# Causal mask by identity matmul, constant rows filled by DMA, V loads from GpSimd, and one-batch FFN groups in a fused attention and FFN kernel

## The chip, the cores and the metric

The kernel runs on 1 core of a Trainium2 chip. The metric is device time in microseconds (us). The profile records one execution. A run is called slow when it lies more than 1.5% above the fastest run of the same kernel; comparisons use fast runs, and differences in us are between means of fast runs. Ratios are the mean time of one kernel's fast runs over the mean of the other's fast runs in the same rounds, so they are not quite the ratio of the times quoted beside them. The kernel before itself took 329.7 to 331.4 us in the several rounds, so a difference between kernels of different rounds is uncertain by some 2 us.

Engine names in profile lines: PE is TensorE, PEld its weight loads, DVE VectorE, ACT ScalarE, POOL GpSimd, SP SyncE. A name with a q (SPq, ACTq) is that engine's sequencer, which here issues transfers.

## The reference

Eight batches of eight heads, 576 positions, head width 64. Attention with a decay from cumulated log f and a causal mask is followed by an FFN with a three-tap convolution and a gate. Abridged:

```python
scores = scale * np.matmul(q, k.transpose(0, 1, 3, 2))
cum = np.cumsum(np.log(np.clip(f, 0.0001, 1.0)), axis=-1)
decay = cum[:, :, :, None] - cum[:, :, None, :]
scores = np.where(causal, -1e9, scores + decay)       # causal: strictly above the diagonal
attn = softmax(scores)
x = np.matmul(attn, v)        # heads put side by side: (8, 576, 512)
h = np.maximum(x @ w_in, 0.0)                         # 512 -> 1024
conv_out = sum(conv_w[k] * shifted(h, k) for k in range(3))
out = (h * sigmoid(conv_out)) @ w_out                 # 1024 -> 512
```

## The kernel before

Work goes by groups of four heads (`hb`, 16 of them) and head pairs (`i`, 32). The q and k of a group are transposed on their way in by a DMA that lays each value into an odd row of a 128-row bf16 tile; the even rows hold what the DMA finds beside it and must become constants. A clamp (a multiply and an add on the 16-bit pattern) does this. Two of the even rows then get the high and low part of cumulated log f, so that one matmul gives score and decay. A ring of four tiles holds the groups.

```python
    def clamp(hb, p, side, eng):
        t = (stq_t, stk_t)[side][hb % RING].bitcast(U16)[:, 2 * p * S:2 * (p + 1) * S]
        eng.tensor_scalar(t, t, lim[:, 2 * side:2 * side + 1], lim[:, 2 * side + 1:2 * side + 2],
                          op0=ALU.mult, op1=ALU.add)

    def rows_of(hb):                       # the rows of cumulated log f, from DRAM
        nc.gpsimd.dma_start(tq[0:1, 0:HS], kd[0:1, c, :].rearrange("j h s -> j (h s)"))
        nc.gpsimd.dma_start(bass.AP(tensor=tk.tensor, ...), kd[:, c, :]...)

    def load_v(b, eng, h0=0, h1=H):        # five DMAs; eng is ScalarE for batch 0, SyncE later
        ...
    # [cut] a mask is a select on GpSimd after the exponential
    def diag_exp(i):
        p_of[i, 3] = pd_pool.tile([128, 1024], FP32, name="p32")
        nc.scalar.activation(p_of[i, 3], sc_of.pop((i, 2)), AF.Exp, scale=SCALE)

    def diag_mask(i):
        p_of[i, 2] = pm_pool.tile([128, 1024], FP16, name="pm")
        nc.gpsimd.affine_select(p_of[i, 2]..., p_of.pop((i, 3))..., pattern=[[0, 8], [1, 128]], base=0,
                                channel_multiplier=-1, compare_op=ALU.is_ge, fill=0.0)
    # [cut] the FFN takes batches in groups (first batch, number)
    GROUPS = [(0, 1), (1, 2), (3, 2), (5, 2), (7, 1)]
```

The order on each engine is fixed when the program is built: each piece of work is a `task` with an estimated cost, the tasks it follows and a key, and a small list scheduler plays them through once.

The softmax here doesn't subtract the row's maximum and nothing guards it: scores larger than these inputs give would overflow.

## Time and profile before

| | before |
|---|---|
| median of 3 runs | 331.68 us (329.85 to 332.91) |
| span of the profiled run | 329.2 us |
| busy PE / DVE / ACT / POOL | 231.0 / 238.5 / 202.3 / 163.4 us |
| first exponential of attention | 23.7 us |

Two parts of the page come back throughout. The first line gives busy time, share of the span and instruction count of each engine. The others give, for each DMA queue, its packets, its megabytes and the time that its packets took as a share of 16 engines' span. Queue q1 carries what SyncE issues, q10 what ScalarE issues, q0 what GpSimd issues.

```profile
PE 231.0 (70%) x2296; PEld 147.6 (45%) x2296; DVE 238.5 (72%) x260; ACT 202.3 (61%) x300; POOL 163.4 (50%) x179
...
q1 hardware_dynamic: 127526, 40.28, 60.9%
q0 software_dynamic: 2528, 2.31, 4.1%
q10 hardware_dynamic: 4872, 1.34, 2.0%
```

Packets in flight together count each in full, so in a short stretch the share can exceed 1.

### The profile page before, as it was taken

Reading aid. Unit: us, or ns where it says so; the run is one execution under the profiler, and the core shown is the slowest. Engines: PE = TensorE matmul, PEld = TensorE weight load, DVE = VectorE, ACT = ScalarE, POOL = GpSimd, SP = SyncE. Lnnn points to the kernel's source line nnn. Section 1 sums busy time; section 2 is a strip of 40 time slices with the busy share of each in tenths; the row PEclk is TensorE's granted clock in tenths of the full one; section 3 lists DMA queues with packets and bytes.
Section 4 is the critical chain, followed back from the end, with each engine's and each line's share of the span. In section 5 each row is a group of like instructions: output and inputs, shape, how many; then the busy total and the mean of one; then the engine's idle time right before and its main releaser. Section 6 shows DMA issues by size and latency. Waiting matters only on the chain. (4 is left out here: it accounts for less than half of the span.)

```text
span 329.2 us, 5881 instructions
## 1 busy us (share of the span) xinstructions
PE 231.0 (70%) x2296; PEld 147.6 (45%) x2296; DVE 238.5 (72%) x260; ACT 202.3 (61%) x300; POOL 163.4 (50%) x179
## 2 busy tenths in 40 slices
PE   0018267567588995196285995699889988889994
PEld 0016155445365663163143663365557554445441
DVE  1606147879897379999999889199956997986720
ACT  2106066569676893275477687098887976565632
POOL 0847262859666749379299989962242100000000
PEclk9999689899879999589699899599999999999998
DMA  9999999779279699669935899411050110121323
GB/s 160 272 190 219 215 216 194 129 118 176 50 119 218 120 205 269 109 105 248 209 60 100 165 215 194 81 65 66 20 149 3 66 64 0 66 96 65 129 112 128
DMA packets 134954, 44.31 MB, mean 135 GB/s; under 512 B 128545, under 2 KB 129709, under 8 KB 134926
## 3 DMA queue, kind: packets, MB, share of 16 engines
q1 hardware_dynamic: 127526, 40.28, 60.9%
q0 software_dynamic: 2528, 2.31, 4.1%
q10 hardware_dynamic: 4872, 1.34, 2.0%
q8 instruction: 18, 0.29, 0.4%
q14 instruction: 10, 0.08, 0.1%
HBM read 14.00 MB, written 9.58 MB: 72 GB/s over the span
## 5 line engine op out<-in xcount | busy, mean ns | idle before, releaser
L368 PE MATMUL mm<-xt,w_in_f 128*128 128x384 f16 (+1 forms) x416 | 77.0, 320 | 8.7 <-ACT ht L381 3.1
L420 PE MATMUL mm<-w_out_f,hg 128*128 128x512 f16 (+1 forms) x296 | 71.7, 391 | 3.3 <-ACT ht L389 2.1
L260 ACT ACTIVATE po<-sc 128x1024 f16<-128x1024 f32 x64 | 64.1, 1028 | 10.5 <-PE sc L254 10.2
L278 POOL TENSOR_SCALAR_AFFINE_SELECT pm<-p 128x1024 f16<-128x1024 f32 x32 | 40.8, 1275 | 46.5 <-ACT p L274 46.5
L398 DVE SCALAR_TENSOR_TENSOR u<-ht,cwt 128x1152 f32<-128x1152 f16 (+1 forms) x40 | 53.8, 1345 | 10.3 <-ACT ht L385 5.2
L411 DVE SCALAR_TENSOR_TENSOR hg<-hg,ht 128x1152 f16<-128x1152 f16 (+1 forms) x40 | 55.3, 1386 | 5.5 <-ACT hg L405 5.4
L405 ACT ACTIVATE hg<-u,cwt 128x1152 f16<-128x1152 f32 (+1 forms) x40 | 42.3, 1062 | 27.6 <-DVE u L400 27.6
L368 PEld LDWEIGHTS <-w_in_f 128*128 128x128 f16 x416 | 39.7, 99 | 33.2 <-issue 14.0
L299 PE MATMUL O<-va,pm 128*128 128x65 f16 x256 | 32.9, 201 | 30.3 <-DVE xn L312 15.7
L400 DVE SCALAR_TENSOR_TENSOR u<-ht,cwt,u 128x1152 f32<-128x1152 f16 (+1 forms) x40 | 51.4, 1284 | 0.8
L254 PE MATMUL sc<-stq,stk 128*128 128x448 bf16 (+3 forms) x256 | 41.3, 292 | 14.1 <-ACT po L260 7.6
L100 POOL TENSOR_SCALAR stk<-stk,lim 128x1152 uint16<-128x1152 uint16 x21 | 43.1, 2052 | 8.8 <-DMA stk<-in_k_dram 8.7
L420 PEld LDWEIGHTS <-hg 128*128 128x128 f16 (+1 forms) x296 | 29.0, 100 | 35.0 <-issue 7.2
L429 ACT ACTIVATE ob<-mm 128x512 f32<-128x512 f32 (+1 forms) x34 | 20.2, 595 | 34.7 <-PE mm L420 27.8
L299 PE MATMUL O<-va,po 128*128 128x65 f16 x640 | 39.2, 200 | 0.0
L299 PEld LDWEIGHTS <-po 128*128 128x128 f16 x640 | 33.2, 102 | 10.5 <-issue 9.0
L299 PEld LDWEIGHTS <-pm 128*128 128x128 f16 x256 | 25.1, 103 | 27.8 <-POOL pm L278 19.6
L274 ACT ACTIVATE p<-sc 128x1024 f32<-128x1024 f32 x32 | 33.0, 1032 | 3.7 <-PE sc L269 3.0
L310 DVE RECIPROCAL rc<-O 128x10 f32<-128x10 f32 x32 | 6.8, 213 | 37.6 <-PE O L299 37.6
L254 PEld LDWEIGHTS <-stk 128*128 128x128 bf16 x256 | 20.4, 104 | 26.8 <-issue 18.2
L100 POOL TENSOR_SCALAR stq<-stq,lim 128x1152 uint16<-128x1152 uint16 x17 | 27.5, 1618 | 0.1
L312 DVE TENSOR_TENSOR xn<-O,rc 128x640 f16<-128x640 f32 x32 | 26.4, 825 | 1.1
(71 smaller groups left out, 248.6 us busy)
## 6 DMA issues: line engine op xcount, KB each, us to landing
out_dram<-ob SPq DMA_DIRECT2D x16, 512.0 KB, 2.8
vf<-in_v_dram SPq DMA_DIRECT2D x28, 256.0 KB, 5.1
vf<-in_v_dram ACTq DMA_DIRECT2D x8, 128.0 KB, 4.8
w_in_f<-in_moe_w_in_dram POOLq DMA_DIRECT2D x1, 1024.0 KB, 9.6
w_out_f<-in_moe_w_out_dram POOLq DMA_DIRECT2D x1, 1024.0 KB, 11.1
vf<-in_v_dram SPq DMA_DIRECT2D x7, 128.0 KB, 5.2
out_dram<-ob SPq DMA_DIRECT2D x3, 256.0 KB, 3.0
xt<-xn SPq DMA_TRANSPOSE x30, 2.6
```

What stands on the lines that cost most here:

```text
L100: eng.tensor_scalar(t, t, lim[:, 2 * side:2 * side + 1], lim[:, 2 * side + 1:2 * side + 2], op0=ALU.mult, op1=ALU.add)
L254: nc.tensor.matmul(sc[:, OFF[m]:OFF[m] + w], tk[:, h * S + 128 * m:h * S + 128 * (m + 1)], tq[:, h * S + 128 * (m + 1):(h + 1) * S], start ...
L260: nc.scalar.activation(p_of[i, s][:, 0:1024], sc_of.pop((i, s)), AF.Exp, scale=SCALE)
L274: nc.scalar.activation(p_of[i, 3], sc_of.pop((i, 2)), AF.Exp, scale=SCALE)
L278: nc.gpsimd.affine_select(p_of[i, 2].rearrange("p (m j) -> p m j", j=128), p_of.pop((i, 3)).rearrange("p (m j) -> p m j", j=128), pattern= ...
L299: nc.tensor.matmul(O[:, s, 65 * Q:65 * (Q + 1)], w, va[:, h, m, :], start=(m == 0), stop=(m == Q))
L368: nc.tensor.matmul(ps[:, 0:w], w_in_f16[:, cc, 128 * ff:128 * (ff + 1)], xt[:, cc, w * t:w * (t + 1)], start=(cc == 0), stop=(cc == NCC - 1))
L398: nc.vector.scalar_tensor_tensor(u, hl, cwt[:, ff, 0:1], hc, op0=ALU.mult, op1=ALU.add)
L400: nc.vector.scalar_tensor_tensor(u, hr, cwt[:, ff, 1:2], u, op0=ALU.mult, op1=ALU.add)
L405: nc.scalar.activation(hgt[g, ff].rearrange("p (a s) -> p a s", s=S), u_of.pop((g, ff)), AF.Tanh, scale=cwt[:, ff, 2:3])
L411: nc.vector.scalar_tensor_tensor(hv, hv, 1.0, hc, op0=ALU.add, op1=ALU.mult)
L420: nc.tensor.matmul(ps[0:n, :], hgt[g, ff][:, 128 * c:128 * c + n], w_out_f16[:, ff, :], start=(ff == 0), stop=(ff == NFF - 1))
```

## The change

The intent is to free GpSimd, and DVE, whose steps are stretched beside it (the prediction shows this). The mask moves to PE: an identity matmul writes a matrix of 0 and -1e6 into PSUM, and the scores accumulate on it. From the fifth group on, the even rows are no longer clamped but overwritten by a DMA from a constant tile (a fill). V loads are issued from GpSimd. FFN groups are mostly of one batch. The start is rearranged.

```diff
-    GROUPS = [(0, 1), (1, 2), (3, 2), (5, 2), (7, 1)]
+    GROUPS = [(0, 1), (1, 1), (2, 1), (3, 1), (4, 2), (6, 1), (7, 1)]
+    def fill(hb, side):
+        t, src = ((stq_t, zq_src), (stk_t, zk_src))[side]
+        t = t[hb % RING]
+        row = t.shape[-1]
+        nc.sync.dma_start(bass.AP(tensor=t.tensor, offset=int(t.offset), ap=[[2 * row, 64], [1, HS]]), src)
-    nc.scalar.dma_start(fsb, f.rearrange("b h s -> (b h) s"))
+    nc.sync.dma_start(fsb, f.rearrange("b h s -> (b h) s"))
     load_qk(0, 0, 2)
     load_qk(0, 2, 2)
-    load_v(0, nc.scalar, 0, HH)
+    load_v(0, nc.gpsimd, 0, HH)
 ... [cut: constants; clamps of the first group on DVE, each pair followed by its row copies]
-    load_v(0, nc.scalar, HH, H)
-    load_qk(1, 0, 4)
+    load_v(0, nc.gpsimd, HH, H)
+    load_qk(1, 0, 4)
 ... [cut: diagonal scores; the tail likewise]
+            nc.tensor.matmul(sc[:, 512 * s:512 * (s + 1)], identb, trib, start=True, stop=False, ...)
             for m in range(4):
                 nc.tensor.matmul(sc[:, 512 * s + 128 * m:512 * s + 128 * (m + 1)],
-                                 tk[:, o:o + 128], tq[:, o:o + 128], start=True, stop=True)
+                                 tk[:, o:o + 128], tq[:, o:o + 128], start=False, stop=m == 3, ...)
-    def diag_mask(i):
-        nc.gpsimd.affine_select(...)
+    def fill_sources():
+        nc.gpsimd.memset(zq_src, 0.0)
+        nc.gpsimd.memset(zk_src, 0.0)
+        nc.gpsimd.memset(zq_src[0:3, :], 1.0)
+        nc.gpsimd.memset(zk_src[0:1, :], -1.0)
+    CLAMPS = 4
+            if hb >= CLAMPS:
+                even.append(task({"SP": 0.6}, [t_fsrc, x], ..., lambda hb=hb, s=s: fill(hb, s), ...))
+            elif hb:
+                even.extend(task({"DVE": 0.55}, [x], ..., lambda ...: clamp(hb, p, s, nc.vector)) for p in range(2))
-                          key + 0.2, lambda b=b: load_v(b, nc.sync), lag=2.0, dma=5.0)
+                                     key + 1.2, lambda b=b: load_v(b, nc.gpsimd), lag=2.0, dma=5.5, behind=last)
```

More of the change, by code (lines that the diff above doesn't have):

```diff
@@ L61 @@
     ident16 = cpool.tile([128, 128], FP16)
+    identb = cpool.tile([128, 128], BF16)
+    trib = cpool.tile([128, 512], BF16)
+    trit = cpool.tile([128, HH * SL], BF16)
+    zq_src = cpool.tile([64, HS], BF16)
+    zk_src = cpool.tile([64, HS], BF16)
     w_in_f16 = cpool.tile([128, NCC, D_FF], FP16)
@@ L101, in clamp, with rows_qk @@
                           op0=ALU.mult, op1=ALU.add)
-    def rows_qk(hb, eng):
+    def rows_qk(hb, eng, h0, nh):
         tq, tk = stq_t[hb % RING], stk_t[hb % RING]
-        c = slice(hb * HH, (hb + 1) * HH)
-        eng.dma_start(tq[0:1, 0:HS], khi_sb[c, :])
-        eng.dma_start(tk[2:3, 0:HS], khi_sb[c, :])
-        eng.dma_start(tk[4:5, 0:HS], klo_sb[c, :])
+        r, c = slice(hb * HH + h0, hb * HH + h0 + nh), slice(h0 * S, (h0 + nh) * S)
+        eng.dma_start(tq[0:1, c], khi_sb[r, :])
+        eng.dma_start(tk[2:3, c], khi_sb[r, :])
+        eng.dma_start(tk[4:5, c], klo_sb[r, :])
+    def fill(hb, side):
[3 more added lines that the diff above has]
+        nc.sync.dma_start(bass.AP(tensor=t.tensor, offset=int(t.offset), ap=[[2 * row, 64], [1, HS]]), src)
     def rows_of(hb):
@@ L136, in cast_v @@
             eng.tensor_scalar(va[:, 2:4, 0:4, 0:64], vf[:, 2:4, 0:4, :], 1.0, 0.0, op0=ALU.mult, op1=ALU.add)
-    nc.scalar.dma_start(fsb, f.rearrange("b h s -> (b h) s"))
+    nc.sync.dma_start(fsb, f.rearrange("b h s -> (b h) s"))
     load_qk(0, 0, 2)
     load_qk(0, 2, 2)
-    load_v(0, nc.scalar, 0, HH)
     nc.gpsimd.iota(lii[:, 0:1], pattern=[[0, 1]], base=0, channel_multiplier=1)
+    load_v(0, nc.gpsimd, 0, HH)
+    nc.gpsimd.memset(trib, -1.0e6)
+    nc.gpsimd.affine_select(trib.rearrange("p (m j) -> p m j", j=128), trib.rearrange("p (m j) -> p m j", j=128),
+                            pattern=[[0, 4], [-1, 128]], base=-1, channel_multiplier=1,
+                            compare_op=ALU.is_ge, fill=0.0)
+    make_identity(nc, ident)
+    nc.gpsimd.tensor_copy(identb, ident)
     nc.vector.memset(one1, 1.0)
@@ L157 @@
     nc.scalar.preload_act_table(AF.Exp)
-    load_v(0, nc.scalar, HH, H)
-    load_qk(1, 0, 4)
     nc.vector.tensor_tensor_scan(cum, one1.broadcast_to((BH, S)), fsb, 0.0, op0=ALU.mult, op1=ALU.add)
-    for t in range(RING):
-        nc.gpsimd.memset(stk_t[t][:, HS:HS + 64], 0.0)
-    clamp(0, 0, 1, nc.gpsimd)
-    clamp(0, 1, 1, nc.gpsimd)
     nc.vector.tensor_scalar(khi_sb, cum, float(-1.0 / SCALE), None, op0=ALU.mult)
@@ L167 @@
                                    op0=ALU.mult, op1=ALU.subtract)
-    clamp(0, 0, 0, nc.vector)
-    clamp(0, 1, 0, nc.vector)
-    rows_qk(0, nc.scalar)
+    for p in range(2):
+        for s in range(2):
+            clamp(0, p, s, nc.vector)
+        rows_qk(0, nc.scalar, 2 * p, 2)
+    for t in range(RING):
+        nc.vector.memset(stk_t[t][:, HS:HS + 64], 0.0)
+    for t in range(2):
+        nc.vector.memset(p4_t[t][:, HH * SL:], 0.0)
+    for t in range(4):
+        nc.vector.memset(po_t[t][:, 1024:], 0.0)
+    load_v(0, nc.gpsimd, HH, H)
+    load_qk(1, 0, 4)
     nc.sync.dma_start(kd[0], khi_sb)
@@ L173 @@
     nc.sync.dma_start(cwrow, moe_conv_w)
-    for t in range(2):
-        nc.gpsimd.memset(p4_t[t][:, HH * SL:], 0.0)
-    for t in range(4):
-        nc.gpsimd.memset(po_t[t][:, 1024:], 0.0)
+    trv = trit.rearrange("p (h j) -> p h j", j=SL)
+    nc.gpsimd.tensor_copy(trv, trib[:, 0:SL].unsqueeze(1).broadcast_to((128, HH, SL)))
     for t in range(3):
@@ L184 @@
         nc.gpsimd.memset(ht_t[t][:, :, HT_W - 1:HT_W], 0.0)
-    make_identity(nc, ident)
     nc.gpsimd.tensor_copy(ident16, ident)
@@ L191 @@
     mm_pool = ctx.enter_context(tc.tile_pool(name="mmp", bufs=2, space=bass.MemoryType.PSUM))
-    pd_pool = ctx.enter_context(tc.tile_pool(name="pdp", bufs=2))
     pm_pool = ctx.enter_context(tc.tile_pool(name="pmp", bufs=2))
@@ L229, in tail_scores @@
         sc = sc_of["t", hb] = sc_pool.tile([128, 1024], FP32, name="sc")
+        nc.tensor.matmul(sc[:, 0:HH * SL], identb, trit, start=True, stop=False, skip_group_check=True)
         for h in range(HH):
@@ L232, in tail_scores @@
             nc.tensor.matmul(sc[:, SL * h:SL * (h + 1)], tk[:, o:o + 128], tq[:, o:o + SL],
-                             start=True, stop=True)
+                             start=False, stop=h == HH - 1, skip_group_check=True)
     def tail_exp(hb):
-        pt = p_of["t", hb] = pd_pool.tile([128, HH * SL], FP32, name="p32t")
-        nc.scalar.activation(pt, sc_of.pop(("t", hb))[:, 0:HH * SL], AF.Exp, scale=SCALE)
-    def tail_mask(hb):
-        nc.gpsimd.affine_select(p4_t[hb % 2][:, 0:HH * SL].rearrange("p (h j) -> p h j", j=SL),
-                                p_of.pop(("t", hb)).rearrange("p (h j) -> p h j", j=SL),
-                                pattern=[[0, HH], [1, SL]], base=0,
-                                channel_multiplier=-1, compare_op=ALU.is_ge, fill=0.0)
+        nc.scalar.activation(p4_t[hb % 2][:, 0:HH * SL], sc_of.pop(("t", hb))[:, 0:HH * SL], AF.Exp, scale=SCALE)
     OFF = {0: 0, 3: 448, 1: 512, 2: 832}
@@ L266, in diag_scores @@
             tq, tk = stq_t[hb % RING], stk_t[hb % RING]
+            nc.tensor.matmul(sc[:, 512 * s:512 * (s + 1)], identb, trib, start=True, stop=False,
+                             skip_group_check=True)
             for m in range(4):
@@ L269, in diag_scores @@
                 nc.tensor.matmul(sc[:, 512 * s + 128 * m:512 * s + 128 * (m + 1)],
-                                 tk[:, o:o + 128], tq[:, o:o + 128], start=True, stop=True)
+                                 tk[:, o:o + 128], tq[:, o:o + 128], start=False, stop=m == 3,
+                                 skip_group_check=True)
     def diag_exp(i):
-        p_of[i, 3] = pd_pool.tile([128, 1024], FP32, name="p32")
-        nc.scalar.activation(p_of[i, 3], sc_of.pop((i, 2)), AF.Exp, scale=SCALE)
-    def diag_mask(i):
         p_of[i, 2] = pm_pool.tile([128, 1024], FP16, name="pm")
-        nc.gpsimd.affine_select(p_of[i, 2].rearrange("p (m j) -> p m j", j=128),
-                                p_of.pop((i, 3)).rearrange("p (m j) -> p m j", j=128),
-                                pattern=[[0, 8], [1, 128]], base=0,
-                                channel_multiplier=-1, compare_op=ALU.is_ge, fill=0.0)
+        nc.scalar.activation(p_of[i, 2], sc_of.pop((i, 2)), AF.Exp, scale=SCALE)
     def pv(i, s):
@@ L461, in task @@
         return len(tasks) - 1
-    room = {"sc": 2, "O": 1, "mm": 2, "pd": 2, "pt": 2, "pm": 2, "xn": 2, "xt": 2, "u": 2, "ht": NHT,
+    def fill_sources():
[4 more added lines that the diff above has]
+    CLAMPS = 4
+    room = {"sc": 2, "O": 1, "mm": 2, "pm": 2, "xn": 2, "xt": 2, "u": 2, "ht": NHT,
             "hg": 2, "ob": 2}
@@ L469 @@
         w_in_f16, moe_w_in.rearrange("(cc p) ff -> p cc ff", p=128)), lag=2.0, dma=6.0)
-    t_wout = task({"POOL": 0.9}, [], 8.0, lambda: nc.gpsimd.dma_start(
-        w_out_f16, moe_w_out.rearrange("(ffc p) dm -> p ffc dm", p=128)), lag=2.0, dma=6.0)
+    t_fsrc = task({"POOL": 1.0}, [], 1.0, fill_sources)
+    last = t_win
     for hb in range(NHB):
-        key = 2 * hb - 4.5
+        key = 2 * hb - 5.5
         ring = [x for j in range(2) for x in t_qk[hb - RING, j]] if hb >= RING else []
@@ L477 @@
         b = hb // 2
-        if hb == 1:
-            for s in range(2):
-                t_load[hb, s] = task({"SP": 0.01}, [], key, lambda: None, lag=5.0 + 2.5 * s)
-        elif hb:
-            for s in range(2):
-                t_load[hb, s] = task({"SP": 2.4}, ring, key + 0.1 * s,
-                                     lambda hb=hb, s=s: load_qk(hb, 0, 4, s), lag=2.0, dma=2.9)
-        else:
-            t_load[hb, 0] = t_load[hb, 1] = None
-        if hb % 2 == 0 and b:
-            t_v[b] = task({"SP": 3.0}, [t_cast[2 * b - j, p] for j in (4, 3) for p in range(2)] if b >= 2 else [],
-                          key + 0.2, lambda b=b: load_v(b, nc.sync), lag=2.0, dma=5.0)
-        elif hb == 0:
-            t_v[0] = None
@@ L492 @@
-        if hb:
-            cl = []
-            for p in range(2):
-                for s in range(2):
-                    cl.append(task({"POOL": 1.35, "DVE": 0.5},
-                                   [t_load[hb, s]], 2 * hb - 3 + 0.2 * (2 * p + s),
-                                   lambda e, hb=hb, p=p, s=s: clamp(hb, p, s, e)))
-            t_rows[hb] = task({"POOL": 1.6}, cl, 2 * hb - 2.2, lambda hb=hb: rows_of(hb), lag=2.3)
-        else:
-            t_rows[0] = None
+        even = []
@@ new lines @@
+        for s in range(2):
+            if hb == 1:
+                x = task({"SP": 0.01}, [], key, lambda: None, lag=4.0 + 3.0 * s)
+            elif hb:
+                last = x = task({"SP": 2.5}, ring, key + 0.1 * s, lambda hb=hb, s=s: load_qk(hb, 0, 4, s),
+                                lag=2.0, dma=2.9, behind=last)
+            if hb >= CLAMPS:
+                even.append(task({"SP": 0.6}, [t_fsrc, x], key + 0.5 + 0.1 * s, lambda hb=hb, s=s: fill(hb, s),
+                                 lag=2.0, dma=0.8))
+            elif hb:
+                even.extend(task({"DVE": 0.55}, [x], 2 * hb - 3 + 0.2 * (2 * p + s),
+                                 lambda hb=hb, p=p, s=s: clamp(hb, p, s, nc.vector)) for p in range(2))
@@ new lines @@
+        if hb % 2 == 0:
+            t_v[b] = None
+            if b:
+                last = t_v[b] = task({"POOL": 4.5}, [t_cast[2 * b - j, p] for j in (4, 3) for p in range(2)] if b >= 2 else [],
+                                     key + 1.2, lambda b=b: load_v(b, nc.gpsimd), lag=2.0, dma=5.5, behind=last)
+        if hb == 3:
+            last = t_wout = task({"POOL": 0.9}, [], key + 1.0, lambda: nc.gpsimd.dma_start(
+                w_out_f16, moe_w_out.rearrange("(ffc p) dm -> p ffc dm", p=128)), lag=2.0, dma=6.0, behind=last)
@@ L502 @@
+        t_rows[hb] = task({"POOL": 1.1}, even, 2 * hb - 3.0, lambda hb=hb: rows_of(hb), lag=2.5) if hb else None
         for p in range(2):
-            t_cast[hb, p] = task({"POOL": 1.1 if p == 0 else 0.6, "DVE": 0.9 if p == 0 else 0.5}, [t_v[b]] + ([t_pv[2 * hb - 5, 1]] if hb >= 3 else []),
-                                 2 * hb - 2.1 + 0.5 * p,
+            t_cast[hb, p] = task({"POOL": 1.1 if p == 0 else 0.65, "DVE": 0.7 if p == 0 else 0.42},
+                                 [t_v[b]] + ([t_pv[2 * hb - 5, 1]] if hb >= 3 else []), 2 * hb - 2.1 + 0.5 * p,
@@ L509 @@
             if p == 0:
-                t_tail = x = task({"PE": 0.13}, [t_rows[hb]], i + 0.02, lambda hb=hb: tail_scores(hb), take="sc")
-                y = task({"ACT": 0.36}, [x], i + 0.02, lambda hb=hb: tail_exp(hb), take="pt", give=[("sc", x)])
-                tail = task({"POOL": 0.5}, [y] + ([t_pv[i - 3, 1]] if hb >= 2 else []), i - 0.5,
-                            lambda hb=hb: tail_mask(hb), give=[("pt", y)])
+                t_tail = x = task({"PE": 0.25}, [t_rows[hb]], i + 0.02, lambda hb=hb: tail_scores(hb), take="sc")
+                tail = task({"ACT": 0.36}, [x] + ([t_pv[i - 3, 1]] if hb >= 2 else []), i + 0.02,
+                            lambda hb=hb: tail_exp(hb), give=[("sc", x)])
             exps = {}
-            x = task({"PE": 0.46}, [t_rows[hb]], i + 0.1, lambda i=i: diag_scores(i), take="sc")
+            x = task({"PE": 0.9}, [t_rows[hb]], i + 0.1, lambda i=i: diag_scores(i), take="sc")
             t_qk[hb, p] = [t_tail, x]
-            y = task({"ACT": 1.02}, [x], i + 0.1, lambda i=i: diag_exp(i), take="pd", give=[("sc", x)])
-            mask = task({"POOL": 1.35}, [y], i - 0.4, lambda i=i: diag_mask(i), take="pm", give=[("pd", y)])
+            mask = task({"ACT": 1.02}, [x], i + 0.1, lambda i=i: diag_exp(i), take="pm", give=[("sc", x)])
             for s in range(2):
@@ L567 @@
                                   give=[("mm", x)]))
-            y = task({"DVE": 0.13 + n / 960.0}, relus + [t_cw], key + 0.15, lambda g=g, ff=ff: conv(g, ff, 0), take="u")
-            x = task({"DVE": 0.13 + n / 960.0}, [y], key + 0.14, lambda g=g, ff=ff: conv(g, ff, 1))
+            y = task({"DVE": 0.15 + n / 960.0}, relus + [t_cw], key + 0.15, lambda g=g, ff=ff: conv(g, ff, 0), take="u")
+            x = task({"DVE": 0.15 + n / 960.0}, [y], key + 0.14, lambda g=g, ff=ff: conv(g, ff, 1))
             x = task({"ACT": 0.19 + n / 1200.0}, [x] + t_tanh[0:1], key - 0.5, lambda g=g, ff=ff: tanh(g, ff),
@@ L572 @@
             t_tanh.append(x)
-            t_gate[g, ff] = task({"DVE": 0.1 + n / 960.0}, [x], key - 0.2, lambda g=g, ff=ff: gate(g, ff),
+            t_gate[g, ff] = task({"DVE": 0.12 + n / 960.0}, [x], key - 0.2, lambda g=g, ff=ff: gate(g, ff),
                                  give=[("ht", t_m1[-nt])])
@@ L592, in play @@
     def play():
-        busy = {"PE": 12.0, "ACT": 11.0, "DVE": 11.0, "POOL": 12.0, "SP": 11.5}
+        busy = {"PE": 11.0, "ACT": 11.0, "DVE": 12.0, "POOL": 14.0, "SP": 14.0}
         ready = {e: [] for e in busy}
-        dma_free, clock = 19.0, 0.0
+        dma_free, clock = 20.0, 0.0
         heap, order = [], []
@@ L640, in play @@
                             continue
-                    if dma and dma_free > clock + 5.0:
+                    if dma and dma_free > clock + 12.0:
                         kept.append((key, k))
-                        heapq.heappush(heap, (dma_free - 5.0, -1, None))
+                        heapq.heappush(heap, (dma_free - 12.0, -1, None))
                         continue
```

## The prediction

> **What bounds the kernel now.** I read the profile from coarse to fine: first the busy tenths per slice, to see whether one engine is the bound throughout; then the busy time of each engine in stretches that I cut at events (first score, first FFN step on DVE, end of attention); then, for each stretch, the groups, the waits and the order of time.
>
> ```profile
> PE   0018267567588995196285995699889988889994
> DVE  1606147879897379999999889199956997986720
> POOL 0847262859666749379299989962242100000000
> DMA  9999999779279699669935899411050110121323
> ```
>
> No engine is full throughout. DMA is full in the first seven slices, DVE is full in the middle, and PE is nearly full only in the last third. The stretches show the same in microseconds (columns: stretch, length, then the busy time of PE, PE's weight loads, DVE, ACT and POOL with instruction counts, then the granted PE clock, the DMA share and GB/s):
>
> ```profile
> 0.00:23.30 23.30, 0.00 (x0) 0.01 (x1) 7.31 (x20) 3.25 (x3) 10.47 (x39) 1.00 1.10 208
> 23.30:52.60 29.30, 18.44 (x233) 14.09 (x234) 10.85 (x23) 14.67 (x19) 14.83 (x17) 0.88 1.20 218
> 52.60:120.00 67.40, 50.97 (x654) 36.98 (x653) 52.08 (x72) 49.80 (x73) 43.99 (x47) 0.92 0.80 138
> 120.00:200.00 80.00, 53.64 (x582) 35.13 (x581) 76.44 (x57) 50.99 (x73) 63.88 (x53) 0.87 0.90 170
> 200.00:260.00 60.00, 49.41 (x496) 31.40 (x495) 46.01 (x42) 44.34 (x66) 28.54 (x24) 0.94 0.32 72
> 260.00:329.20 69.20, 58.52 (x339) 30.04 (x337) 45.84 (x50) 39.20 (x69) 1.64 (x1) 0.98 0.23 85
> ```
>
> PE does nothing for 23.3 us. From 120 to 200 us it is busy 54 of 80 us while DVE is busy 76 of 80: DVE is the bound there. From 260 us on, POOL is idle and PE is busy 85%. The waits name what starts the two early gaps:
>
> ```profile
> PE sc L232 <- DMA stk<-klo_sb: 23.3, 1, 23.3
> ...
> ACT L156 <- DMA vf<-in_v_dram: 6.5, 1, 6.5
> PE sc L232 <- DMA stq<-kd: 6.2, 1, 6.2
> ```
>
> The first score waits for the rows of cumulated log f. Those wait in ACT's queue behind V loads, and so did the logarithm. The second four heads wait another 6.2 us for rows whose transfer was issued at 32 us, because POOL's clamps come after its masks.
>
> Is the DVE work of the middle real work? Compare one group over the whole run with the same group after 262 us, when POOL is silent, then look at the worst case in order of time (start, length):
>
> ```profile
> L411 DVE SCALAR_TENSOR_TENSOR hg<-hg,ht 128x1152 f16<-128x1152 f16 x24 | 40.6, 1691 | 2.1 <-ACT hg L405 2.1
> ```
>
> ```profile
> L411 DVE SCALAR_TENSOR_TENSOR hg<-hg,ht 128x1152 f16<-128x1152 f16 x6 | 8.1, 1353 | 1.7 <-ACT hg L405 1.7
> ```
>
> ```profile
> 123.98 10.83 DVE L136 TENSOR_SCALAR va<-vf 128x512 f16<-128x512 f32 x1
> 124.31 2.58 POOL L100 TENSOR_SCALAR stq<-stq,lim 128x1152 uint16<-128x1152 uint16 x2
> ...
> 126.88 1.29 POOL L100 TENSOR_SCALAR stk<-stk,lim 128x1152 uint16<-128x1152 uint16 x1
> ```
>
> A V cast whose median on DVE is 424 ns shows 10.83 us while POOL runs masks and clamps one after another. PE then waits 10.7 us for the normalisation behind it. So a good part of DVE's busy time is waiting for POOL.
>
> **What the Trainium skill says.** "SBUF — State Buffer", section "Who interferes with whom", says that DVE and GpSimd share one port pair as an exclusive lock: a DVE tensor_scalar in a two-port mode contends with GpSimd, and a DVE instruction with two SBUF inputs contends with a GpSimd instruction that reads SBUF. The trace agrees: the scalar_tensor_tensor steps and the casts are the stretched ones, and the normalisation, which reads PSUM, has the same 825 ns beside POOL and without it. "DMA: Bandwidth & Descriptors", section "SWDGE vs HWDGE vs iDMA", says that a transfer issued from GpSimd has its descriptors written by GpSimd. This matters because V loads move there. The trace has only few such issues, some 0.5 us each for the row copies and 0.95 to 0.98 for the weights. "TensorE: Matmul & The Clock Gate", section "Back-to-back issue gap", gives N/2.4 + 2.5 ns for a warm isolated gap, 216 ns for 512 columns. The trace agrees: 64 second-FFN matmuls of 512 columns took 13.95 us in the chain that ended last, 218 ns each.
>
> **The change part by part.**
>
> Masks. It removes 32 mask selects at 1275 ns (40.8 us) and 16 at 813 ns (13.0 us) from POOL, and one engine hop between each diagonal exponential and its PV product. PE waited for those selects 13.0 us in all, with a further 19.6 us at the weight load of the same products, which overlaps it. The exponential itself is unchanged in size (1028 against 1032 ns for f16 or f32 output). It adds, per head pair, two identity matmuls of 512 columns, 64 x 0.218 = 14.0 us of PE, and 16 of 256 columns, about 0.11 each, 1.7 us. PE will be the scarce engine, so I count these 15.7 us on the path.
>
> Clamps. 38 of 64 are on POOL, 43.1 + 27.5 = 70.6 us, and 26 on DVE. After it 16 remain, all on DVE at 0.57 us: 9 us against 26 x 0.57 = 15 without contention. In their place are 24 fills by DMA of 64 rows x 4608 B = 295 KB. At the 213 GB/s of the early stretches I estimate 1.4 us each, 33 us of transfer over some 200 us. They start only at the fifth group of four heads, where DMA is no longer saturated in every slice, and have two groups' time to land. I put nothing of it on the path.
>
> DVE contention. The excess is count x (mean of the group - mean or median when alone). For the three wide steps: 24 x (1.651-1.411) + 24 x (1.534-1.414) + 24 x (1.691-1.353) = 16.8 us. For the narrow ones, 16 x ((0.885-0.814) + (0.911-0.817) + (0.927-0.755)) = 5.4. For the L136 casts, 10 x (1.677-0.424) = 12.5. For clamps, 15 x 0.281 + 11 x 0.176 = 6.2. For the other casts, 6 x 0.49 + 6 x 0.14 = 3.8. The sum is 44.7 us of DVE's 238.5. POOL keeps only V casts, so I leave 5 us of it.
>
> FFN groups of one batch. Two pairs become four singles. Per pair and FFN slice, DVE pays 2 x (0.814+0.817+0.755) - (1.411+1.414+1.353) = 0.59 us, over 16 slices 9.5 us. ACT pays 0.16 for relu (4 x 0.410 - 3 x 0.493) and 0.29 for tanh, 16 x 0.45 = 7.3 us, and 1.2 for two more evictions. PE pays two more output chunks, 2 x 8 x 0.218 = 3.5 us, and 64 x (4 x 0.161 - 3 x 0.196) = 3.6 us for narrower tiles. In return the FFN of a batch becomes ready earlier, which gives PE something to do sooner.
>
> Sums. PE 231.0 + 15.7 + 7.1 = 254. DVE 238.5 - 44.7 + 5 - 6 + 9.5 = 202. ACT 202.3 + 8.5 = 211. POOL 163 - 124 + V loads. If one V transfer costs about what a weight transfer costs (0.95 us, an estimate), 45 of them are 43 us, so POOL has about 80. PE becomes the bound, and no other engine is near it.
>
> Start. The f load goes first on SP's queue, and ACT no longer issues V. The chain is logarithm, scan 1.35, high part 1.39, low part 0.75, clamps 4 x 0.57, rows. The second k transpose landed at 11.8 us; add about 1.2 us for the last clamps and about 4 us for issue and landing of the rows (before: issued from 17.4, landed by 23.3). First score at about 17 us instead of 23.3. The 6.2 us wait for the second rows should mostly go, as its clamps no longer queue behind masks. The stretch stays DMA-bound (share 1.20), so I take 10 us for both together: the work done by 52.6 us is done by 42.
>
> Rest. PE work after that point was 231.0 - 18.4 = 213, and becomes about 213 + 21 = 234, less some 3 us because the granted clock (0.87 in the middle) should rise as gaps shorten: 231. PE utilisation there was 77% (213 of 276.6). In the two last stretches it was 82 and 85%, and 90% in the best parts (36.0 of 40 us from 240 to 280, 17.9 of 20 from 220 to 240). With DVE freed I take 88%: 231/0.88 = 262. The time is 42 + 262 = 304, and the reported time is 1 to 2 us above the span: **305 us**.
>
> **The rivals.** (1) **PE takes it back.** The 22.8 us that PE gains are on the path, and the order of a fixed schedule keeps utilisation at 80%: 42 + 231/0.80 = 331. For it speaks that PE has only two FFN result buffers and is still idle 15% of the quiet end. Against it speaks that the middle's idle time is named: waits for DVE and POOL. (2) **DMA becomes the bound.** Fills (33 us) are added to a queue that is already 90% busy from 120 to 200 us, and V loads come late from POOL. Attention would still end near 255 us and the time be about 320. Against it: the share falls to 0.32 once loads are done, and PE's waits for DMA are the two early ones. (3) **Only the start counts**, because freed DVE time was hidden: 331.7 - 10 + part of 22.8, about 325 to 335. Against it: DVE is 96% busy for 80 us while PE is 67% busy. (4) **Better than expected**: utilisation 93% gives 42 + 248 = 290.
>
> **Range and chances.** Utilisation 93 to 83% spans 290 to 320 us, and I take that as the range. Faster by over 2% means below 325 us, which needs only 82%. I give it 0.88. Within 2% has 0.10 (rivals 1 and 3), slower 0.02.
>
> **What would show it.** In the profile after: PE busy near 250, and above 85% of each stretch between 60 us and the end; DVE near 200, its wide steps at 1.35 to 1.45 us and no cast over 2 us; POOL below 100; first score near 17 us; no single PE wait on a mask. The prediction is wrong if PE busy stays below 80% in the middle (then look for waits on rows, fills or V loads), if DVE steps are still stretched (then descriptor writing or the casts hold the ports), or if the identity matmuls cost well above 0.22 us each.

## The result

The changed kernel takes 360.70 us (median of 4 runs, 357.20 to 368.66, one of them slow), against 331.51 us for the kernel before in the same rounds. The ratio is 1.0847, interval 1.0735 to 1.0960: **slower by 8.5%**.

The profiled run after is fast, with a span of 355.5 us. Its engines and DMA queues, read as those of before:

```profile
PE 255.6 (72%) x2456; PEld 162.0 (46%) x2456; DVE 207.3 (58%) x315; ACT 205.7 (58%) x329; POOL 85.8 (24%) x134
...
q1 hardware_dynamic: 96742, 39.25, 58.9%
q0 software_dynamic: 5552, 11.75, 19.2%
q10 hardware_dynamic: 24, 0.01, 0.0%
```

The engines did what was foretold: PE 256, DVE 207, POOL 86. But the packet time rose from 221 us to 78.1% of 355.5 = 278 us. The busy tenths in 40 slices of the same run (8.9 us each) show where:

```profile
PE   0000728698497978995571999899799769899985
...
DVE  5380352569901897192670388831289998676950
...
DMA  8999997999488999999989999998830000212123
```

DMA is at 8 or 9 in 25 of the first 27 slices, while PE and DVE have holes there. The busy times in the stretches that the prediction used for before (columns as there):

```profile
0.00:23.30 23.30, 0.37 (x1) 0.10 (x1) 13.44 (x18) 3.25 (x3) 21.60 (x44) 1.00 1.07 159
23.30:52.60 29.30, 8.49 (x113) 6.01 (x114) 9.80 (x36) 6.20 (x7) 7.52 (x10) 0.96 1.09 208
52.60:120.00 67.40, 54.45 (x561) 35.30 (x559) 34.47 (x61) 41.94 (x67) 20.18 (x27) 0.86 0.92 171
120.00:200.00 80.00, 56.26 (x608) 38.33 (x605) 44.00 (x66) 48.84 (x79) 23.23 (x34) 0.88 1.06 162
```

From 23.3 to 52.6 us PE did 8.5 us of work where it had done 18.4. From 120 to 200 us DVE is relieved, 44 us busy for 76, but PE is still only 56 of 80 us busy, and the DMA share went from 0.90 to 1.06. So the bound moved from DVE to the transfers. The waits, as before (us in total, times, longest), name them:

```profile
DVE rc L319 <- PE O L308: 72.3, 19, 13.2
...
POOL stk L131 <- DMA stk<-zk_src: 34.7, 6, 14.0
POOL va L147 <- DMA vf<-in_v_dram: 30.1, 2, 23.2
PE sc L252 <- DMA stk<-klo_sb: 24.2, 2, 15.5
```

GpSimd waits for the fills of k (`zk_src`) before it may issue row copies, and for V before it casts. DVE waits for PE in its normalisation, and PE for what those two deliver. The worst place, in order of time (start, length), with the chain of waits below it:

```profile
144.56 4.36 POOL L140 DMA_DIRECT2D vf<-in_v_dram  x5
...
153.56 22.90 SPq L99 DMA_TRANSPOSE stq<-in_q_dram  x1
```

```profile
147.33 24.59 DMA vf<-in_v_dram
```

GpSimd issues five V transfers at 144.6 us. The one issued at 147.3 us lands 24.6 us later, and beside them SyncE needs 22.9 us to get one transposing load of q out. V took 8.0 us to land in the median (24.6 at most), against 5.1 (10.2) before.

The start is late too, by the order of time of DVE, ACT and POOL:

```profile
15.37 6.55 DVE L107 TENSOR_SCALAR stq<-stq,lim 128x1152 uint16<-128x1152 uint16 x1 [1.92 <-DMA stq<-in_q_dram]
...
15.68 2.04 POOL L473 MEMSET zq_src<- 64x2304 bf16 x1
...
23.14 0.57 ACTq L116 DMA_DIRECT2D stk<-klo_sb  x1
...
31.18 0.57 ACTq L114 DMA_DIRECT2D stq<-khi_sb  x1
...
37.62 0.38 ACT L256 ACTIVATE pr<-sc 128x256 f16<-128x256 f32 x1 [31.39 <-PE sc L252]
```

A clamp that takes 0.57 us alone takes 6.55 us beside GpSimd's memsets of the fill sources. The row copies of the second head pair go out only at 31 us, and the first exponential starts at 37.6 us, where it had started at 23.7.

What the change meant to gain is there. The widest DVE steps show it, in groups that keep shapes apart:

```profile
L420 DVE SCALAR_TENSOR_TENSOR hg<-hg,ht 128x1152 f16<-128x1152 f16 x8 | 10.8, 1349 | 0.0
```

Its mean was 1691 ns beside GpSimd before; now it is 1349 ns, like the 1353 of the quiet end.

**How far the transfers reach.** I cut both runs where the last transposing load of q or k has landed, by the last step of that load's completion counter in the trace (columns as in the stretches above). First the kernel before:

```profile
0.00:207.30 207.30, 125.00 (x1480) 87.42 (x1480) 153.39 (x176) 122.83 (x173) 140.47 (x157) 0.91 0.94 171
```

Then the kernel after:

```profile
0.00:244.00 244.00, 161.89 (x1761) 108.39 (x1762) 131.50 (x228) 133.91 (x207) 84.20 (x131) 0.92 1.03 178
```

The DMA share up to that point was high already, 0.94, and rises to 1.03; the point comes 36.7 us later. What follows it takes 111.5 us against 121.9. The 26.3 us between the spans are thus lost while loads run, and some 10 us are won back after them.

### The profile page after: what moved, and what is told of

Read it like the earlier page. It is cut to its first block, busy times and chain, and to the rows that moved or that the text cites. A ratio compares the mean times of both kernels' runs of the same rounds, so it can differ in the third digit from the quotient of the medians.

```text
span 355.5 us, 6212 instructions
## 1 busy us (share of the span) xinstructions
PE 255.6 (72%) x2456; PEld 162.0 (46%) x2456; DVE 207.3 (58%) x315; ACT 205.7 (58%) x329; POOL 85.8 (24%) x134
## 4 chain that ended last, share of the span: by engine, by line
PE 27%; DMA 24%; DVE 13%; SPq 13%; issue 12%; ACT 6%; POOL 4%; ACTq 0%; POOLq 0%; DVEq 0%
PE mm L429 10%; DMA vf<-in_v_dram 10%; SPq L99 7%; PE mm L377 6%; SPq L340 5%; DMA stk<-kd 4%; PE O L308 3%; DVE u L409 3%; DVE u L407 3%; DVE hg L420 3%; DMA xt<-xn 3%; PE sc L267 3%; DVE xn L321 2%; ACT hg L414 2%; ACT ob L438 2%
## 5 line engine op out<-in xcount | busy, mean ns | idle before, releaser
L377 PE MATMUL mm<-xt,w_in_f 128*128 128x288 f16 (+1 forms) x480 | 84.1, 311 | 28.5 <-DMA xt<-xn 10.2
L377 PEld LDWEIGHTS <-w_in_f 128*128 128x128 f16 x480 | 46.8, 103 | 52.0 <-issue 35.5
L407 DVE SCALAR_TENSOR_TENSOR u<-ht,cwt 128x576 f32<-128x576 f16 (+1 forms) x56 | 50.4, 904 | 10.4 <-ACT ht L390 9.1
L414 ACT ACTIVATE hg<-u,cwt 128x576 f16<-128x576 f32 (+1 forms) x56 | 47.3, 851 | 15.4 <-DVE u L409 15.2
L420 DVE SCALAR_TENSOR_TENSOR hg<-hg,ht 128x576 f16<-128x576 f16 (+1 forms) x56 | 46.5, 840 | 9.7 <-ACT hg L414 9.5
L409 DVE SCALAR_TENSOR_TENSOR u<-ht,cwt,u 128x576 f32<-128x576 f16 (+1 forms) x56 | 50.5, 906 | 1.1
L390 ACT ACTIVATE ht<-mm 128x288 f16<-128x288 f32 x96 | 39.6, 425 | 16.1 <-PE mm L377 14.8
L290 ACT ACTIVATE pm<-sc 128x1024 f16<-128x1024 f32 x32 | 32.9, 1027 | 19.4 <-PE sc L284 19.3
L140 POOL DMA_DIRECT2D vf<-in_v_dram x45 | 38.0, 851 | 1.1 <-issue 1.0
L256 ACT ACTIVATE pr<-sc 128x256 f16<-128x256 f32 x16 | 6.1, 383 | 45.4 <-PE sc L252 45.3
```

Source lines behind the costliest of these rows:

```text
L140: eng.dma_start(vf[0:n, h0:h1, kb, :], bass.AP(tensor=v.tensor, offset=base + h0 * S * D + kb * 128 * D, ap=[[D, n], [S * D, h1 - h0], [1, ...
L377: nc.tensor.matmul(ps[:, 0:w], w_in_f16[:, cc, 128 * ff:128 * (ff + 1)], xt[:, cc, w * t:w * (t + 1)], start=(cc == 0), stop=(cc == NCC - 1))
L390: nc.scalar.activation(ht[:, 0, 1 + w * t:1 + w * (t + 1)], ps[:, 0:w], AF.Relu)
L407: nc.vector.scalar_tensor_tensor(u, hl, cwt[:, ff, 0:1], hc, op0=ALU.mult, op1=ALU.add)
L409: nc.vector.scalar_tensor_tensor(u, hr, cwt[:, ff, 1:2], u, op0=ALU.mult, op1=ALU.add)
L414: nc.scalar.activation(hgt[g, ff].rearrange("p (a s) -> p a s", s=S), u_of.pop((g, ff)), AF.Tanh, scale=cwt[:, ff, 2:3])
```

## The experiments

My theory after the result: the transfers pace the first 244 us, and two parts of the change lengthen them, the fills and the move of V to GpSimd's queue. Rivals: the smaller FFN groups; the chain load, fill, row copy, score as a chain rather than as traffic; the start alone; the mask on PE.

Twelve kernels ran, all correct, three rounds each. All that follow are edits of the kernel after, except the one marked. Packet time is worked out as above from each profiled run (e5's is of a slow run, the rest are fast). The figures in brackets after a ratio are its 95% interval.

| kernel | edit | fast runs, mean us (number) | ratio to before (interval) | first exponential us | packet time us |
|---|---|---|---|---|---|
| before | | 331.4 (4) | | 23.7 | 221 |
| after | | 359.5 (3) | 1.085 (1.074 to 1.096) | 37.6 | 278 |
| e1 | V from SyncE | 335.5 (4) | 1.018 (1.011 to 1.024) | 27.5 | 261 |
| e2 | no fills | 341.8 (2) | 1.037 (1.029 to 1.045) | 45.4 | 254 |
| e3 | groups of before | 355.8 (3) | 1.076 (1.066 to 1.086) | 47.4 | 282 |
| e4 | e1 and e2 | 304.7 (3) | 0.924 (0.916 to 0.933) | 26.9 | 231 |
| e5 | e4, V after batch 0 from GpSimd | 322.5 (2) | 0.975 (0.968 to 0.982) | 31.7 | 244 |
| e6 | e4, V after batch 0 from ScalarE | 345.7 (3) | 1.045 (1.036 to 1.054) | 26.9 | 226 |
| e7 | e4 with fills nobody waits for | 332.4 (2) | 1.005 (0.998 to 1.011) | 27.0 | 257 |
| e9 | e4 without fill sources | 304.2 (3) | 0.925 (0.919 to 0.932) | 26.6 | 228 |
| e10 | before, with the mask part alone | 320.9 (2) | 0.970 (0.959 to 0.980) | 23.3 | 222 |
| e11 | e9 with V lower in the text | 306.5 (3) | 0.924 (0.916 to 0.933) | 27.0 | 233 |
| e12 | e11, groups of before | 319.2 (4) | 0.965 (0.958 to 0.971) | 26.3 | 228 |
| e13 | e9, V of batch 0 from ScalarE | 315.0 (4) | 0.953 (0.949 to 0.957) | 35.3 | 229 |

### e1: V from SyncE

```diff
-    load_v(0, nc.gpsimd, 0, HH)
+    load_v(0, nc.sync, 0, HH)
-    load_v(0, nc.gpsimd, HH, H)
+    load_v(0, nc.sync, HH, H)
-                                     key + 1.2, lambda b=b: load_v(b, nc.gpsimd), ...
+                                     key + 1.2, lambda b=b: load_v(b, nc.sync), ...
```

> The changed kernel with one edit: the V loads are issued from SyncE at the same places of the program instead of from GpSimd. Theory Q (V on the GpSimd queue runs beside the transposing loads and slows both: V landed in 8.0 us at the median and 24.6 at most, against 5.1 and 10.2 before; first scores at 37 us; PE 9 of 20 us busy from 180 to 200): about 335 us, first scores below 28 us, V landing back at 5 to 6 us, no PE gap of 20 us in the middle. Theory F (the fills load a DMA system that was full already): within 2% of the changed kernel (361). A rival against Q: SyncE's queue becomes longer, so loads behind V come later and nothing is won.

335.5 us: some 24 us of the loss come back by a change of the issuing engine alone. At the start one sees how. In the kernel after, the fourth load of the first group (order of time of SyncE):

```profile
7.88 5.15 SPq L99 DMA_TRANSPOSE stk<-in_k_dram  x1
```

In e1 the same load:

```profile
5.83 1.43 SPq L99 DMA_TRANSPOSE stk<-in_k_dram  x1
```

On SyncE, V comes after q and k in one queue. On GpSimd the V of batch 0 went out from 1.5 and 8.4 us on, and SyncE's transposing loads, which the first scores need, went out more slowly beside it. The first exponential comes 10 us earlier in e1. The Trainium skill, "DMA: Bandwidth & Descriptors", section "Issuing engines are not separate DMA queues", says that transfers of all issuing engines run on the same 16 DMA engines and interleave there. The runs agree: a third issuing engine gave no transfer capacity, and with V moved to it the packet time was 278 us for 261.

### e2: no fills

```diff
-    CLAMPS = 4
+    CLAMPS = 16
```

> The changed kernel with the constant of clamped groups at 16 instead of 4: no fills, all 64 clamps on VectorE (48 more at 0.57 us, 27 us of VectorE). Theory F: 36 us of transfer time on 16 engines go (1536 packets of 4608 B at 380 ns), all of it in the DMA-full stage from 65 to 265 us, so 325 to 340 us. Theory Q: at most 10 us faster, the late start at 37 us and the gap near 180 us stay.

341.8 us: 18 us come back although DVE has 48 more clamps to do and its busy time is 229.9 us for 207.3. Neither theory alone foretold it: F said 325 to 340 us, Q at most 10 us back.

### e3: the groups of before

```diff
-    GROUPS = [(0, 1), (1, 1), (2, 1), (3, 1), (4, 2), (6, 1), (7, 1)]
+    GROUPS = [(0, 1), (1, 2), (3, 2), (5, 2), (7, 1)]
```

> The changed kernel with the FFN groups of the kernel before. Theories F and Q both: within 2% of the changed kernel, PE busy lower by 5 to 7 us and VectorE by about 10, since transfers set the pace until 260 us. A theory G (the one-batch groups and the order that follows cost the time): 340 or less.

355.8 us, 1% below the kernel after. The groups are not the cause of the loss.

### e4: V from SyncE and no fills

The edits of e1 and e2 together.

> The changed kernel with both edits: V from SyncE and no fills. Theories F and Q together: the working of the prediction holds again and the time is 300 to 315 us, PE over 82% busy after the first 40 us. If PE work or the order of the schedule is what costs (theory G), it stays above 330.

304.7 us. The two edits return 55 us together where they returned 24 and 18 alone: without fills V's move is worth 37 us (341.8 - 304.7), and with V on SyncE the fills are worth 31 (335.5 - 304.7). The same cut at the last transposing load, now at 197.7 us:

```profile
0.00:197.70 197.70, 148.46 (x1742) 103.04 (x1757) 151.00 (x266) 136.44 (x210) 51.52 (x92) 0.97 1.06 188
```

The share is 1.06. By this sign transfers still pace attention, but the loads end 46.3 us sooner than in the kernel after, and the packet time is 47 us less. What follows takes 106.0 us.

### e5: only the middle V from GpSimd

e4, with batch 0's V from SyncE and the V of later batches back on GpSimd.

> As e4 (no fills, V from SyncE, 306 us), but V of batches 1 to 7 goes back to GpSimd's queue; only batch 0's V stays on SyncE. Without fills, V on GpSimd (e2) cost 39 us over e4. Theory start (it costs only by holding up the first rows, whose scores come at about 27 us in e4): 306 to 312. Theory both (some 18 us at the start, the rest in the middle): 320 to 330.

322.5 us, so V's 37 us split in two: 19 for batch 0's loads (e2 to e5) and 18 for the others (e5 to e4). Some 5 of the 18 are again the start: GpSimd sends V of the next batch at 15.3 us, ahead of loads that the first groups need, and the first exponential comes at 31.7 us instead of 26.9. For the rest the packet records show a change in the packets themselves. GpSimd moves V in packets of 4096 B, where SyncE moves it in packets of 256 B. The 256 B packets of SyncE's queue, nearly all of transposing loads, took 48 ns on average when they started beside a V packet in flight (56 ns in the kernel after), and 23 to 24 ns otherwise. Over the whole run this is 25.9 ns for 23.5 in e4; times 92160 packets over 16 DMA engines that is 14 us, about the 13 us by which the packet time rose. V's own packets took no longer: 2304 at 370 ns in the kernel after are 53 us for each DMA engine, and 36864 at e4's mean of 23.5 ns would be 54.

### e6: the middle V from ScalarE

e4, with `nc.scalar` for the V of later batches.

> As e5, but the middle V loads go to ScalarE's queue: hardware descriptors as on SyncE, yet a second stream beside the transposing loads as on GpSimd. If a second stream is what hurts in the middle: 320 to 330, as e5. If it is GpSimd's own descriptors, or GpSimd's order of work: 306 to 314 (some 4 us of issuing per batch on ScalarE is in that).

This was to tell whether a second issuing stream as such does the harm. By its time it cannot, for ScalarE itself was held up by issuing (order of time of ACT):

```profile
171.90 9.32 ACTq L140 DMA_DIRECT2D vf<-in_v_dram  x4
181.33 0.41 ACT L390 ACTIVATE ht<-mm 128x288 f16<-128x288 f32 x1 [8.95 <-DMA vf<-in_v_dram]
```

At 345.7 us it is 41 us slower than e4 with less packet time (226 us), and the 35 issues of V took 50 us of ScalarE. As a time the run is a miss for its question, and a warning: an engine that computes should not issue such transfers beside a busy queue. The packet records answer a part: V came from ScalarE in packets of 256 B, and SyncE's 256 B packets took 30 ns beside them and 23.2 over the whole run (e4 23.5). So a second queue of small packets lengthened the loads little. Packet size and GpSimd's way of issuing are not told apart.

### e7: fills that nobody waits for

e4 with 24 transfers of the fill's size and place in SyncE's queue, which write into a spare tile.

```diff
+    def junk_fill(hb, side):
+        nc.sync.dma_start(bass.AP(tensor=zk_src.tensor, offset=int(zk_src.offset) + side * HS,
+                                  ap=[[2 * HS, 64], [1, HS]]), zq_src)
+            if hb >= 4:
+                task({"SP": 0.6}, [t_fsrc, x], key + 0.5 + 0.1 * s, lambda hb=hb, s=s: junk_fill(hb, s), ...)
```

> As e4, with clamps on VectorE, and 24 transfers of the size of the fills issued at the places of the fills into a tile that nobody reads. Theory traffic (the fills cost by the 34 us of engine time they take in a full DMA system and by the places they take in SyncE's queue): 325 to 335, as e1. Theory chain (they cost because the row copies wait for a load, then a fill, then their own landing): 306 to 312.

332.4 us, near e1, where the fills are waited for (335.5). So the fills cost by being in the queue, 28 us over e4, and the chain through them adds at most a few us. By the packet records the fills of the kernel after are 1536 packets of 4608 B at 380 ns, 1536 x 0.380 / 16 = 36.5 us for each DMA engine; the idle ones took 35.3. The run does not tell their bytes from their places in SyncE's issue order.

### e9: no fill sources

e4 with `t_fsrc = None`, which takes the four memsets away.

> As e4, without the four memsets on GpSimd that make the sources of the fills, which nothing reads there. In e4 they run from 7.2 to 15.4 us and VectorE's first clamps, 0.57 us of work, take 6.02 and 2.35 us beside them. If the two block each other and this stands on the path: first scores 6 to 8 us earlier, near 19 us, and 297 to 301 us. If the q and k loads or the row copies end the wait anyway: no change.

304.2 us, no gain over e4 beyond what repeats differ by. In e4 the memsets had stretched two clamps to 6.02 and 2.35 us; in e9 all four take 0.56 to 0.58. The blocking is real. It agrees with the Trainium skill, "SBUF — State Buffer", section "Who interferes with whom", which gives a tensor_scalar of DVE in a two-port mode and GpSimd one port pair as an exclusive lock. But it lay off the path here: the clamps of the first group were done by 11.2 us, and the row copies went out at the same time as in e4, 18 to 19 us.

### e10: the mask part alone, on the kernel before

The identity matmuls and their constants put into the kernel before, the selects taken out, nothing else.

> The kernel before with the mask part alone: identity matmuls on PE, no selects on GpSimd; loads, clamps, V casts, groups as before. If the mask part is worth what the prediction says (54 us off GpSimd, its share of VectorE's 45 us of waiting, 16 us more PE work in a stage where PE had idle time): 310 to 322, VectorE busy 210 to 220. If GpSimd's clamps alone keep VectorE blocked, or PE takes it back: 328 to 338.

320.9 us, 3% faster. PE's busy time is 244.7 us for 231.0, and DVE's 226.1, above the 210 to 220 expected. A likely reason, not tested, is that clamps are still on GpSimd and still stretch DVE's steps (groups, shapes apart):

```profile
L399 DVE SCALAR_TENSOR_TENSOR u<-ht,cwt,u 128x1152 f32<-128x1152 f16 x24 | 41.8, 1744 | 0.4
```

The three wide steps together take 4.79 us, against 4.88 before and 4.18 with GpSimd silent.

### e11: V below the row copies in the text

e9 with both V loads of batch 0 written after the row copies of the first group.

> As e9 (V from SyncE, no fills, no memsets of sources, 305 us), with batch 0's V loads written after the row copies in the program. SyncE's own order of issue is the same; only the completion counters change: of eight counters that the hardware-queue transfers take in turn, the row copies then reuse those of the f and q/k loads, not those of V. Theory counter (in e9 the first row copy is issued at 18.1 us though its clamp ended at 8.5, because it waits for a V load to land): row copies issued near 9 to 12 us, first scores near 16, 293 to 299 us. Theory full DMA (the copies would land late anyway, or the second group's loads set the pace): first scores earlier but the time within 1% of 305.

The built program has the instruction order and the waits of e9. It is an unintended repeat: 306.5 against 304.2 us is the size of what repeats differ by.

### e12: the groups of before, in the freed kernel

e11 with the groups of before.

> As e11 with the FFN groups of the kernel before. The working of the prediction put the one-batch groups at 7 us of PE and 9.5 of VectorE against an earlier start of each FFN: if PE is the bound now, 3 to 8 us faster than e11; if transfers pace the attention until 220 us and the FFN fills in, the one-batch groups win, and this is 3 to 10 us slower.

319.2 against 306.5 us: here the one-batch groups are worth 12.7 us, where in the kernel after (e3) they were worth nothing. DVE pays 6 us for them (221.1 against 215.0).

### e13: batch 0's V from ScalarE, after its row copies

```diff
-    load_v(0, nc.sync, 0, HH)
     ...
-    load_v(0, nc.sync, HH, H)
+    load_v(0, nc.scalar, 0, HH)
+    load_v(0, nc.scalar, HH, H)
```

> The kernel without fills, without fill sources and with V on SyncE, but the two V loads of batch 0 issued from ScalarE after its row copies. In e9 and e11 the row copies were issued at 18 us although the clamps were done at 11, and the first scores of the tail came at 26 us. If the row copies were held back by completion counters that they share with the V loads ahead of them, they are issued soon after the clamps now and the first scores come well before 26 us. Theory A, the start is on the path: 295 to 301 us. Theory B, the transposing loads of the groups that follow pace attention in any case, so an earlier first group only waits for the second: within 1 to 2% of the 305 to 308 us of e9 and e11. If V of batch 0 comes too late for the first casts, the gain is lost there, and the wait of the casts for their loads would show it.

315.0 us, slower than e9 and e11, a miss. In e9 the first row copy went out late (order of time of ACT):

```profile
18.09 1.36 ACTq L114 DMA_DIRECT2D stq<-khi_sb  x1
```

In e13:

```profile
8.10 1.22 ACTq L114 DMA_DIRECT2D stq<-khi_sb  x1
...
19.04 0.57 ACTq L116 DMA_DIRECT2D stk<-klo_sb  x1
...
23.07 10.41 ACTq L140 DMA_DIRECT2D vf<-in_v_dram  x9
...
35.27 0.38 ACT L256 ACTIVATE pr<-sc 128x256 f16<-128x256 f32 x1 [29.05 <-DMA vf<-in_v_dram]
```

The theory of the counters held for the first two copies. Each DMA of SyncE and ScalarE takes one of eight completion counters in turn and waits, in the built program, for that counter's last user; with V out of the way they went out at 8.1 and 9.4 us. The third copy still had to wait until 19.0 us, for the counter of the next group's q load. Then ScalarE was held by its own V loads until 35.2 us: the ten issues took 5.7 us by their records, the other 6.5 were waits, since each V load too waits for its counter. This answers whether the start is on the path, though by a loss: at the same packet time (229 against 228 us), a first exponential 8.7 us later than in e9 (8.3 than in e11) made the kernel 10.8 us slower than e9 and 8.5 slower than e11. Whether an earlier start would gain as much is not tried.

## Why the prediction was wrong

**The step that failed** is the one that put transfers off the path. For the fills it says "I put nothing of it on the path". For V it counts only GpSimd's time to issue (43 us estimated, 38.0 measured by the row of V issues). Rival 2, "DMA becomes the bound", is what happened. It was set aside because "PE's waits for DMA are the two early ones"; that was true only while DVE was slow enough to hide the queue. The prediction had the share of 0.90 from 120 to 200 us in hand, and added work to the queue while it shortened the time around it. There was no room: up to the last load of q and k the share was 0.94 before, and in e4, with the same loads and nothing added, it is 1.06, where the engines wait less for each other. The "about 320" of that rival was also too low: it had attention end near 255 us, and the last product of attention starts at 288 us (264 before).

**The size of the fills** was right: 33 us estimated, 36.5 measured, and 26 to 30 us in packet time (e4 to e7 and e1). What failed is its place. The same microseconds show in the time: 28 and 31.

**V on GpSimd** was missed but for rival 2's remark that V would come late. It cost 24 us beside the fills and 37 without them: half by the start, where V overtook the loads of q and k, and half in the middle.

**The start** was to come 6 us earlier, first score at 17 us. The first row copy of the kernel after did go out at 8.4 us, but the last at 33. e9 shows for e4 that the clamps were not what held it, and e1 that most of the delay came with V from GpSimd. The prediction's chain lacks a wait: in the built program of the kernel after, the third and fourth row copies wait for the completion counters of the next group's q and k loads (the counters are explained at e13). Beside V, SyncE was done issuing these at 18.8 and 26.1 us, and the copies went out at 23.1 and 31.2. Even the best start of the runs with the new order, 26.3 us (e12), is later than the 23.7 of before; where V is on SyncE, the counters shared with V loads are one cause (shown in e13 for two of six copies).

**The engine sums** were nearly right: PE 254 predicted and 255.6 measured, DVE 202 and 207.3, ACT 211 and 205.7, POOL about 80 and 85.8. The 44.7 us of DVE's waiting for GpSimd were real: the wide steps fell to 1.35 to 1.42 us, as foretold, and no cast took over 2 us. The identity matmuls added 13.7 us to PE in e10, 15.7 predicted. The cost of smaller groups was put too high for ACT (8.5 predicted, 1.8 between e12 and e11). For PE it stays open (7.1 predicted): busy time is the same in e12 and e11, but at granted clocks of 0.95 and 0.98, and 9.5 us more in the kernel after than in e3, at 0.93 and 0.94.

**305 us reached without the two parts.** e4 takes 304.7 us. That is luck and not the predicted chain come true, for two errors cancel. After 60 us its stretch reads:

```profile
60.00:303.70 243.70, 216.92 (x2135) 139.36 (x2146) 199.62 (x290) 184.16 (x303) 31.76 (x49) 0.98 0.68 135
```

PE is busy 216.9 of 243.7 us, 89%, where the prediction took 88%. But the start is 10 us later than predicted, and PE has 240.6 us of work rather than 254, perhaps since its granted clock is higher (0.98 after 60 us; before had 0.92 there). e4 is balanced rather than free: its share of DMA is 1.06 as long as loads of q and k run.

**The balance of the 29 us lost.** e4 shows that the rest of the change is worth 25 us; the fills took 31 (e4 to e1) and V on GpSimd another 24 (e1 to after), which together is the 55 from 304.7 to 359.5 us.

**Best version.** e4 and e9 beat both kernels, by 7.5% against the kernel before and by 15% against the kernel after. They differ by less than repeats do.

**What stays open.** Why V from GpSimd costs some 13 us in the middle beyond the later start: longer packets of the transposing loads were seen, of about that sum, and e6 speaks against the second queue as such, but no run moves V from GpSimd in small packets. For the fills, bytes are not told from places in SyncE's order. And 305 us is not shown to be the floor, since the start of e9 still waits for row copies at 18 us.

## What to carry to other kernels

Before adding a transfer as a free replacement for computing, read the DMA share of the stretch it falls in, against the time that stretch will have after the change: here a queue at 0.9 hid nothing once the engine in front of it got faster. Loads that are needed later belong in the same in-order queue behind those that are needed first, not on another engine from where they overtake. If two parts of a change fill the same queue, undo them together as well as singly: here they gave back 24 and 18 us alone and 55 together.

## What the Trainium skill lacked or had wrong

- "DMA: Bandwidth & Descriptors", section "Issuing engines are not separate DMA queues", says that a second issuing engine only saves issue time, which it calls usually small beside the DMA. It has no number for what the choice costs when loads that are needed later overtake from another queue: V from GpSimd instead of SyncE cost 24 us with fills and 37 us without.
- The same section, on issue time, which it calls usually small: beside SyncE's loads four issues of V held ScalarE for 9.3 us, and all 35 took 50 us (e6), in a kernel 41 us slower than the one it was made from.
- The same page has no number for what large packets of another queue do to transposing loads in flight: 256 B packets of SyncE's queue took 48 ns on average beside V packets of 4096 B, and 24 ns otherwise (e5).
- "SBUF — State Buffer", section "Who interferes with whom", agrees on the lock but gives no size for a memset on GpSimd: beside memsets of some 2 us each, a 0.57 us clamp on DVE took 6.55 us (after), as it had to outlast about three of them.
- None of the pages cited here has the wait for shared completion counters of these built programs: row copies ready at 8 us went out at 18 us (e9) behind V loads that they had nothing to do with.
